# A transformer block on one Trainium2 core: the key weights are loaded through ScalarE's DMA queue instead of SyncE's

## The chip, the cores and the metric

The kernel runs on one core of a Trainium2 chip. The core has five engines with an instruction stream each: TensorE (PE, matrix multiplication; its weight loads are listed as PEld), VectorE (DVE), ScalarE (ACT), GpSimd (POOL) and SyncE (SP). Transfers between HBM and the on-chip memory SBUF are moved by 16 DMA engines. An instruction on SyncE's or ScalarE's stream issues such a transfer; the two streams feed separate DMA queues, which the profile calls q1 (SyncE) and q10 (ScalarE), and both queues are served by the same 16 DMA engines.

The metric is the device time of one execution in microseconds (us). Nine executions of the kernel before took between 219.12 and 220.82 us, with a median of 219.65 us.

## The reference, cut to what matters

One transformer block over 2048 tokens of width 512, in bf16: a modulated layer norm and a linear attention with 32 heads whose features are a softmax of a small projection and of its negative, then a second modulated layer norm and a gated MLP.

```python
mod = (silu(c) @ w_mod).reshape(1, 6, 1, -1)       # sa, ca, ga, sb, cb, gb
h = layernorm(x) * (1 + ca) + sa
# attention A(h)
q, k, v = split(h @ wqkv)                          # 32 heads of 16
pq, pk = q @ w_phi, k @ w_phi                      # per head, 16x16
phi_q = concat(softmax(pq), softmax(-pq))
phi_k = concat(softmax(pk), softmax(-pk))
kv, z = phi_k.T @ v, phi_k.sum(tokens)
o = (phi_q @ kv) / (phi_q @ z + 1e-6)
x = x + ga * (o @ wo)
h = layernorm(x) * (1 + cb) + sb
x = x + gb * ((sigmoid(h @ w_gate) * (h @ w_up)) @ w_down)
```

The part of this that the change touches is the middle third of `wqkv`, columns 512 to 1023: the key weights, 512 x 512 in bf16, 512 KB.

## The kernel before, in words

The 2048 tokens are 16 tiles of 128. The kernel never computes k itself. It folds the key weights and w_phi into one matrix first, so that pk = h @ wqk_f, and does the same for the queries later. Its first 12 us do this:

- **Loads.** ScalarE issues two small ones: `c_row` (1 KB) and `wp_sb` (w_phi, 16 KB in rows of 32 bytes, lines 493 and 495), and then loads its activation table (line 496). SyncE issues the large ones, in this order: x0a (x of tiles 0 and 1, 256 KB), wk (the key weights into the second half of `wqk_sb`, 512 KB, line 923), x0b (tiles 2 and 3, 256 KB), the two halves of the modulation weights wm00 and wm01 (512 KB each, line 921), x1 (tiles 4 to 7), wv (the value weights), wq (the query weights) and x2 (tiles 8 to 11), 512 KB each. One row of x, wk, wv or wq is 1 KB in a transfer, one of wm00 and wm01 is 2 KB.
- **Warm-up.** PE multiplies zeros (`warm`, line 971) from 1.2 us on, and a few more such products stand between the real ones.
- **Fold.** PE transposes the key weights in 16 blocks (`tp_w`, line 1002); DVE and ACT copy the result from PSUM to `wT_sb` (lines 1008 and 1006). POOL makes the block-diagonal `bd` out of `wp_sb` (line 954). PE multiplies `wT_sb` by `bd` (`fold_ps`, line 1019), and ACT and DVE copy that to `wqk_f` (lines 1025 and 1027).
- **Modulation and layer norm.** DVE takes statistics of each x tile (`st`, line 1043), DVE, ACT or POOL normalises it (`xn`), the tile is transposed on PE (`tp_h`, line 1087) or by a DMA transpose that SyncE issues (line 1079), and the modulation (`modc`, out of wm00 and wm01, line 983) is applied on the way to `h1T`.

Then K and V of each tile are computed by PE (lines 1114 and 1118), the features by ACT, DVE and POOL, and summed into `kvacc`; the queries, the attention output, the second norm and the MLP follow.

The order of the work is set when the program is built. A planner (class `Graph`, line 291) takes each task with its engines, an assumed cost, what it reads and writes, and a due time, the due times being shifted by a table (`DUE`); it runs a list schedule with these numbers, and `emit` (line 530) calls the tasks' functions in that order. From then on each engine executes its stream in order and waits by semaphores only for what an instruction reads. A load task costs SyncE 0.45 in the planner and has a size, from which the planner works out a landing time. The three ScalarE instructions at lines 493 to 496 are not in the plan; they are written out ahead of it.

Transfers signal through eight semaphores that are handed out in turn over the transfers of both queues. A transfer that gets a semaphore for the second time waits at its issue until that semaphore's earlier transfer has landed; for x2 the earlier transfer is `wp_sb`.

Of the kernel before, what the change touches and what calls it, by code (L numbers as in the profile page):

```python
# [17 lines left out]
S, D, H, DH, F = 2048, 512, 32, 16, 1376  # L18
# [407 lines left out]
def kernel(  # L426
# [5 lines left out]
    pe, act, dve, pool, sp = nc.tensor, nc.scalar, nc.vector, nc.gpsimd, nc.sync  # L432
# [39 lines left out]
    wqk_sb = cst.tile([P, KT, 2 * D], BF16, name="wqk_sb")  # L472
# [15 lines left out]
    wqkv_v = A_wqkv.rearrange("(j p) n -> p j n", p=P)  # L488
# [2 lines left out]


    act.dma_start(c_row[:], c)
    with nc.allow_non_contiguous_dma(reason="small w_phi load"):
        act.dma_start(wp_sb[:], A_w_phi.rearrange("(kt hl) d f -> (hl d) kt f", hl=8))
    act.preload_act_table_set("natural_log_exp_and_others")
# [416 lines left out]
    def load(name, key, fn, nbytes, due, rel=0.0):  # L913
        G.add("ld_" + name, {"SP": 0.45}, fn, w=key, due=due, rel=rel, nbytes=nbytes)

    K1 = 1024.0
    def load_x(nm, a, b, due):
        load(nm, [("x", t) for t in range(a, b)], lambda e: sp.dma_start(x_sb[:, a:b, :], x_v[:, a:b, :]), 128 * (b - a) * K1, due, rel=max(0.0, due))

    def load_wm(i, due):  # L920
        load(f"wm0{i}", [("wmod0", i)], lambda e: sp.dma_start(wmod_sb[:, 2 * i:2 * i + 2, 0:1024], wmod_v[:, 2 * i:2 * i + 2, 0:1024]), 512 * K1, due)
    load_x("x0a", 0, 2, -20.0)
    load("wk", ["wk"], lambda e: sp.dma_start(wqk_sb[:, :, D:2 * D], wqkv_v[:, :, D:2 * D]), 512 * K1, -19.0)
    load_wm(0, -18.5)
    load_wm(1, -18.0)
    load_x("x0b", 2, 4, -17.0)
# [375 lines left out]
```

## Time and profile before

| | |
|---|---|
| median of 9 executions | 219.65 us |
| the profiled execution: its time | 219.98 us |
| its span, first to last instruction | 218.1 us |
| PE busy | 204.3 us, 94% of the span |
| DVE busy | 169.5 us, 78% |
| ACT busy | 111.1 us, 51% |
| POOL busy | 95.7 us, 44% |
| moved by DMA | 19.02 MB, 87 GB/s over the span |

Times in the profile are counted from the span's start. A timeline line reads: start, duration, engine, source line, operation, destination<-source, sizes, count, and in brackets how long the engine was idle before it and what released it; "SPq" and "ACTq" are the issue of a transfer on SyncE and ScalarE. A line of waits reads: who waited, for whom, us in total, times, longest. A window line reads: the stretch, its length, the busy time and the number of instructions of PE, PEld, DVE, ACT and POOL, then the mean clock granted to PE (1.00 is full), the busy share of the DMA engines and the GB/s that they moved. The chain is followed back from the last instruction to what released each step.

### The profile page before, as it was taken

How to read it: one execution, taken by the hardware profiler on the slowest of the kernel's cores; microseconds unless marked ns; L12 is line 12 of the kernel's file. 1: busy time of each engine (PE TensorE's matmuls, PEld its weight loads, DVE VectorE, ACT ScalarE, POOL GpSimd, SP SyncE). 2: the span in 40 equal slices, each digit the busy share in tenths (PEclk: the TensorE clock that was granted, in tenths of full speed). 3: DMA queues.
4: the chain of work that ended last, by engine and by line, in shares of the span. 5: the costliest groups of instructions: out<-in, count | busy, mean ns of one | idle time of the engine just before them, and what ended most of it. 6: DMA issues, size and time to landing. Idle time of an engine off the chain costs nothing.

```text
span 218.1 us, 4243 instructions
## 1 busy us (share of the span) xinstructions
PE 204.3 (94%) x1494; PEld 113.9 (52%) x1519; DVE 169.5 (78%) x425; ACT 111.1 (51%) x268; POOL 95.7 (44%) x121
## 2 busy tenths in 40 slices
PE   7995999999999999999997799999999999999990
PEld 2632555564566587868754344554444444444550
DVE  3899999999679998788789999999869872333430
ACT  3797899999858984234642133352233523115100
POOL 4367999999999665813312602233104100000000
PEclk9998899999999999999999999999999999999999
DMA  5998982992000210341311210224111221000011
GB/s 162 366 270 222 325 202 51 329 385 66 0 3 3 48 27 3 75 72 26 73 48 50 48 29 0 48 47 122 2 48 27 48 67 57 0 18 6 6 60 47
DMA packets 32511, 19.02 MB, mean 87 GB/s; under 512 B 21761, under 2 KB 30434, under 8 KB 32482
## 3 DMA queue, kind: packets, MB, share of 16 engines
q1 hardware_dynamic: 31952, 18.65, 32.3%
q8 instruction: 14, 0.23, 0.4%
q14 instruction: 15, 0.12, 0.2%
q10 hardware_dynamic: 530, 0.02, 0.1%
HBM read 11.58 MB, written 2.10 MB: 63 GB/s over the span
## 4 chain that ended last, share of the span: by engine, by line
PE 78%; DVE 10%; DMA 4%; issue 2%; ACT 1%; POOL 1%; SPq 0%; DVEq 0%; POOLq 0%; ACTq 0%
PE g_ps L841 16%; PE y_ps L864 15%; PE u_ps L841 15%; PE k_ps L1114 6%; PE a_ps L752 6%; PE q_ps L1188 6%; PE v_ps L1118 4%; DMA wqk_sb<-in_A_wqkv_dram 2%; DMA h1T<-xn 2%; PE num L719 2%; PE kvacc L544 2%; DVE u L710 1%; DVE m L660 1%; PE num L643 1%; POOL phi L1136 1%
## 5 line engine op out<-in xcount | busy, mean ns | idle before, releaser
L845 ACT ACTIVATE tg<-g_ps 128x512 bf16<-128x512 f32 (+3 forms) x66 | 29.3, 454 | 58.7 <-PE g_ps L841 34.1
L850 DVE SCALAR_TENSOR_TENSOR wmod_sb<-tg,u_ps 128x512 bf16<-128x512 bf16 (+5 forms) x66 | 32.0, 501 | 16.0 <-PE u_ps L841 9.0
L864 PE MATMUL y_ps<-wd_sb,wmod_sb 128*128 128x512 bf16 (+2 forms) x179 | 41.2, 366 | 0.4
L743 POOL TENSOR_TENSOR o<-u 128x512 bf16<-128x512 f32 x14 | 17.7, 1271 | 33.4 <-DVE u L710 24.0
L841 PEld LDWEIGHTS <-wu_sb 128*128 128x128 bf16 (+1 forms) x264 | 23.2, 100 | 17.1 <-DVE u L710 0.7
L841 PEld LDWEIGHTS <-wg_sb 128*128 128x128 bf16 (+1 forms) x264 | 23.0, 100 | 17.5 <-issue 1.4
L1136 POOL TENSOR_TENSOR phi<-e,ks 128x1024 bf16<-128x1024 bf16 (+2 forms) x22 | 31.5, 1454 | 0.4
L841 PE MATMUL g_ps<-wT_sb,wg_sb 128*128 128x512 bf16 (+3 forms) x130 | 25.1, 325 | 1.4 <-DVE u L710 1.1
L864 PEld LDWEIGHTS <-wmod_sb 128*128 128x128 bf16 (+1 forms) x187 | 17.9, 98 | 16.1
L841 PE MATMUL u_ps<-wT_sb,wu_sb 128*128 128x512 bf16 (+3 forms) x130 | 24.9, 325 | 0.1
L841 PE MATMUL u_ps<-wqk_sb,wu_sb 128*128 128x128 bf16 (+5 forms) x132 | 20.8, 290 | 0.2 <-DVE u L710 0.2
L841 PE MATMUL g_ps<-wqk_sb,wg_sb 128*128 128x128 bf16 (+5 forms) x130 | 20.5, 289 | 0.1
L873 DVE TENSOR_TENSOR ot<-y_ps,x 128x512 bf16<-128x512 f32 (+1 forms) x17 | 11.2, 657 | 11.5 <-PE y_ps L864 11.5
L1133 DVE TENSOR_REDUCE ks<-e 128x64 f32<-128x1024 bf16 (+2 forms) x22 | 19.5, 902 | 0.7 <-ACT e L1130 0.7
L1118 PE MATMUL v_ps<-wv_sb,h1T 128*128 128x512 bf16 x61 | 16.4, 388 | 2.1 <-ACT h1T L1094 1.2
L1130 ACT ACTIVATE e<-k_ps 128x512 bf16<-128x512 f32 (+2 forms) x44 | 17.9, 499 | 0.2 <-PE k_ps L1114 0.2
L1193 ACT ACTIVATE eT<-q_ps 128x512 bf16<-128x512 f32 x32 | 17.0, 628 | 1.5 <-PE q_ps L1188 1.0
L1114 PE MATMUL k_ps<-wqk_f,h1T 128*128 128x512 bf16 x61 | 16.5, 395 | 0.2
L752 PE MATMUL a_ps<-wo_sb,oT 128*128 128x512 bf16 x62 | 16.2, 379 | 0.1
L1188 PE MATMUL q_ps<-h1T,wqk_f 128*128 128x512 bf16 x62 | 15.5, 379 | 0.1
L1043 DVE BATCH_NORM_STATS2 st<-x_sb 128x6 f32<-128x512 bf16 x16 | 10.7, 671 | 2.7 <-DMA x_sb<-in_A_x_dram 2.7
L1177 POOL TENSOR_TENSOR wd_sb<-wd_sb,wmod_sb 128x512 bf16<-128x512 bf16 x11 | 12.5, 1169 | 0.0
(146 smaller groups left out, 300.3 us busy)
## 6 DMA issues: line engine op xcount, KB each, us to landing
wmod_sb<-in_w_mod_dram SPq DMA_DIRECT2D x4, 512.0 KB, 6.2
out_dram<-ot SPq DMA_DIRECT2D x15, 128.0 KB, 1.8
x_sb<-in_A_x_dram SPq DMA_DIRECT2D x3, 512.0 KB, 7.8
wg_sb<-in_B_w_gate_dram SPq DMA_DIRECT2D x1, 1376.0 KB, 6.6
wu_sb<-in_B_w_up_dram SPq DMA_DIRECT2D x1, 1376.0 KB, 9.5
wd_sb<-in_B_w_down_dram SPq DMA_DIRECT2D x1, 1280.0 KB, 13.3
wqk_sb<-in_A_wqkv_dram SPq DMA_DIRECT2D x2, 512.0 KB, 7.0
wmod_sb<-in_w_mod_dram SPq DMA_DIRECT2D x1, 1024.0 KB, 6.6
```

The costliest lines, as they stand in the source:

```text
L743: G.add(f"o{t}", {"POOL": 1.3, "DVE": 0.62}, lambda e, ub=ub, o=o: engine(e).tensor_tensor(o[:], ub[0][:].rearrange("p h d -> p (h d)"), u ...
L752: pe.matmul(ap_[:], lhsT=oT[:, j, :], rhs=wo_sb[:, j, :], start=(j == 0), stop=(j == KT - 1))
L841: pe.matmul(ps[:fsz, 0:n], lhsT=w[:, j, ft * P:ft * P + fsz], rhs=h[:, j, 0:n], start=(j == 0), stop=(j == KT - 1))
L845: G.add(f"tg{k}.{ft}", {"ACT": 0.13 + n * 0.00083}, lambda e, tg=tg, g_ps=g_ps, fsz=fsz, n=n: act.activation(tg[:fsz, 0:n], g_ps[:fsz, 0:n ...
L850: dve.scalar_tensor_tensor(hm_all[:fsz, hm[k].slot, ft, 0:n], tg[:fsz, 0:n], 1.0, u_ps[:fsz, 0:n], op0=ALU.add, op1=ALU.mult)
L864: pe.matmul(y[:, 0:c1 - c0], lhsT=hm_all[:fsz, hm[k].slot, ft, tl * P:(tl + 1) * P], rhs=wd_sb[:fsz, ft, c0:c1], start=(ft == 0), stop=(ft ...
L1114: pe.matmul(kp[:], lhsT=h1T[:, j, t * P:(t + 1) * P], rhs=wqk_f[:, j, D:2 * D], start=(j == 0), stop=(j == KT - 1))
L1118: pe.matmul(vp[:], lhsT=h1T[:, j, t * P:(t + 1) * P], rhs=wv_sb[:, j, :], start=(j == 0), stop=(j == KT - 1))
L1130: act.activation(ee[:, ha:hb, s, :], kp[:, ha * DH:hb * DH].rearrange("p (h j) -> p h j", j=DH), ACT.Exp, scale=1.0 - 2.0 * s)
L1133: dve.tensor_reduce(ks[:, ha:hb].rearrange("p h s -> p (h s)"), ee[:, ha:hb].rearrange("p h s j -> p (h s) j"), axis=AX.X, op=ALU.add)
L1136: pool.tensor_tensor(ph[:, ha * 32:hb * 32].rearrange("p (h j) -> p h j", j=DH), ee[:, ha:hb].rearrange("p h s j -> p (h s) j"), ks[:, ha: ...
L1188: pe.matmul(qp[:], lhsT=wqk_f[:, j, blk * P:(blk + 1) * P], rhs=h1T[:, j, cq * 512:(cq + 1) * 512], start=(j == 0), stop=(j == KT - 1))
```

## The change

The key weights' load is taken out of SyncE's stream and written out on ScalarE's, between its two small loads. The planner's task `ld_wk` stays, with its cost and size, but emits nothing, so that the planner makes the same order as before.

```diff
     act.dma_start(c_row[:], c)
+    act.dma_start(wqk_sb[:, :, D:2 * D], wqkv_v[:, :, D:2 * D])
     with nc.allow_non_contiguous_dma(reason="small w_phi load"):
         act.dma_start(wp_sb[:], A_w_phi.rearrange("(kt hl) d f -> (hl d) kt f", hl=8))
     act.preload_act_table_set("natural_log_exp_and_others")
...
     load_x("x0a", 0, 2, -20.0)
-    load("wk", ["wk"], lambda e: sp.dma_start(wqk_sb[:, :, D:2 * D], wqkv_v[:, :, D:2 * D]), 512 * K1, -19.0)
+    load("wk", ["wk"], lambda e: None, 512 * K1, -19.0)
     load_wm(0, -18.5)
```

On SyncE the order is now x0a, x0b, wm00, wm01, x1, wv, wq, x2; on ScalarE it is c_row, wk, wp_sb, the table. All other instructions of all engines stand in the order of before. The semaphores are handed out in turn as before; x2 now shares its semaphore with wk, and waits at its issue for wk's landing instead of that of `wp_sb`.

## The prediction

> **What bounds the kernel now.** I read the page first (PE is busy for 94% of the span, so what the first stage loses is not made up by spare time later unless PE or its feeders have some), then the chain of the first 22 us, then the timeline and the waits of the first 12 us, and the windows for how full the DMA engines and each engine are. The chain:
>
> ```profile
> 1.32 4.74 DMA wqk_sb<-in_A_wqkv_dram
> 6.06 0.05 issue
> 6.11 0.91 PE tp_w L1002 x12
> ...
> 8.92 0.46 PE fold_ps L1019 x8
> 9.38 0.02 issue
> 9.41 0.48 DVE wqk_f L1027
> ...
> 13.94 4.12 DMA h1T<-xn
> ```
>
> The reader is to see that the kernel starts on exactly the load that is moved: wk, issued at 1.32, landed at 6.06, and PE, DVE, POOL and a DMA transpose follow without a gap worth naming. Timeline and waits give the two inputs of the fold, wk and `wp_sb`:
>
> ```profile
> 0.79 0.53 ACTq L493 DMA_DIRECT2D c_row<-in_c_dram  x1
> 1.32 0.45 SPq L923 DMA_DIRECT2D wqk_sb<-in_A_wqkv_dram  x1
> 1.35 0.45 ACTq L495 DMA_DIRECT2D wp_sb<-in_A_w_phi_dram  x1
> 1.83 1.28 ACT L496 ACT_TABLE_LOAD   x1 [1.83 <-issue]
> ...
> 6.11 0.91 PE L1002 MATMUL tp_w<-ident,wqk_sb 128*128 128x128 bf16 x12
> 6.87 1.15 POOL L954 TENSOR_TENSOR bd<-wp_sb,bmask 128x512 bf16<-128x512 bf16 x1 [3.21 <-DMA wp_sb<-in_A_w_phi_dram]
> 8.76 1.06 PE L1019 MATMUL fold_ps<-bd,wT_sb 128*128 128x128 bf16 x16
> 9.41 1.29 DVE L1027 CAST wqk_f<-fold_ps 128x512 bf16<-128x512 f32 x2 [0.33 <-PE fold_ps L1019]
> ```
>
> ScalarE's second issue starts at 1.35, as early as SyncE's second at 1.32: the change buys no earlier issue. `bd` ends at 8.02, 0.74 us before the fold at 8.76. The windows:
>
> ```profile
> 2.00:3.00 1.00, 1.00 (x4) 0.38 (x3) 0.00 (x0) 1.00 (x1) 0.83 (x7) 1.00 0.90 249
> 3.00:4.00 1.00, 1.00 (x6) 0.17 (x5) 0.35 (x1) 0.11 (x1) 0.66 (x7) 1.00 0.59 120
> 4.00:5.00 1.00, 1.00 (x7) 0.43 (x8) 0.96 (x3) 0.47 (x3) 0.00 (x0) 1.00 1.10 351
> 5.00:6.00 1.00, 1.00 (x3) 0.09 (x1) 0.90 (x6) 0.68 (x3) 0.00 (x0) 1.00 1.16 334
> 6.00:7.00 1.00, 0.89 (x14) 0.85 (x14) 0.51 (x3) 0.63 (x1) 0.13 (x1) 1.00 1.07 377
> 7.00:8.00 1.00, 1.00 (x11) 0.57 (x8) 0.97 (x4) 0.87 (x2) 1.00 (x1) 1.00 1.07 393
> 8.00:9.00 1.00, 1.00 (x12) 0.64 (x11) 0.97 (x4) 0.30 (x1) 0.02 (x1) 1.00 1.03 369
> ...
> 20.00:25.00 5.00, 4.95 (x26) 2.51 (x26) 4.61 (x13) 4.12 (x13) 5.00 (x5) 0.66 1.11 323
> ```
>
> From 4 us on one queue keeps all 16 DMA engines full; only 3 to 4 us is thin. The last column added up (GB/s times 1 us is kB, with 16 kB before 2 us) is 385 kB by 4 us, 736 by 5, 1070 by 6, 1447 by 7, 1840 by 8, 2209 by 9.
>
> **The change part by part.**
>
> *SyncE loses one issue (0.45 us).* x0b and the rest are issued 0.5 us earlier. With the engines full that moves no byte sooner by itself: 0. x2 now waits for wk instead of `wp_sb`; behind it on SyncE stand only the transposes at 12.58, and its bytes queue behind wq (issued 4.87, landed 9.3 us later), so a wait of even 5 us is covered: 0.
>
> *ScalarE gains one issue (0.45 us).* The table load moves from 1.83 to 2.33 and ends at 3.6; ScalarE's next instruction started at 4.22, after a wait for PE: covered, with 0.6 us to spare.
>
> *wk shares instead of queueing.* Before, the bytes ahead of and with wk's last were x0a 262 kB, wk 524, c_row and `wp_sb` 17: 803 kB, reached at 5.2 us on the curve; it landed at 6.06, so 0.86 us passes from last byte to landing. Now x0a no longer stands ahead of wk, but all of SyncE's queue runs beside it. Low bound: wk starts at 2.45 (x0a's bytes began about 1.1 us after its issue, between 1.75 and 2.0, and wk is issued at 1.35), the queues share byte by byte, and the second queue fills the thin stretch. Then 128 kB have moved at 2.45, twice 524 follow: 1176 kB, at 6.3 us, less 0.6 us for the filled stretch, plus 0.86: 6.55, that is +0.5. High bound: ScalarE's second transfer starts as late as `wp_sb`'s did (5.4 us from issue to landing for 16 KB; in the trace's packet records its first packet runs at 3.86 us) and shares packet by packet, against wm00 and wm01 with their 2 KB rows. Then 262 + 262 + 524 + 1048 = 2096 kB must move: 8.7 + 0.86 = 9.55, that is +3.5. I take sharing packet by packet from 3.0 us, because `wp_sb`'s records do just that (one of its packets every 48 ns on an engine, between wk's of 46 ns): x0b's 262 kB beside half of wk, then 524 kB of wm beside the other half, 262 + 524 + 262 + 524 = 1572 kB, at 7.3 us; plus 0.86, less 0.2 for part of the thin stretch: wk lands at 8.0, **+1.9 us**. Below nothing is nearly excluded: PE's last warm-up product starts at 5.37 and such products follow each other every 0.43 us, so `tp_w` cannot start before 5.8, a gain of 0.3 at most.
>
> The Trainium skill, in "DMA: Bandwidth & Descriptors", under "Issuing engines are not separate DMA queues", says that transfers from different engines run on the same 16 DMA engines and interleave, and that a second issuer saves only the sequencer's time. The windows agree, at 334 to 393 GB/s from one queue. By that rule the change would gain at most an issue, 0.45 us, and here not that; it speaks against the change.
>
> *`wp_sb` goes behind wk* in ScalarE's queue. It cannot land before wk; low bound 0.3 after it. High bound: each DMA engine has 32 of its packets and each waits for one 2 KB packet of the other queue, 83 ns at the 393 GB/s shared by 16: 2.7 us after wk. I take 1.3: 9.3. `bd` (1.15) then ends at 10.5, where PE, running `tp_w` to fold in 2.65 us as before (6.11 to 8.76), reaches the fold at 8.05 + 2.65 = 10.7. So it is just covered; at the high bound `bd` ends at 11.95 and the fold is 3.2 late instead of 1.9.
>
> *PE's clock.* PE is idle from 5.8 to 8.0. After 16 to 20 us, in which PE is busy 1.47 of 4 us, the granted clock averages 0.66 in 20 to 25: 1.7 us of clock lost. A gap of 2.2 us may or may not do the same: 0 to +1.7. I take +0.3, as the gap is shorter and much of what follows waits for DVE.
>
> *What of it reaches the end.* The fold's delay goes to DVE's copies (9.41), the norm's scalars, `xn` and the DMA transposes (issued 12.58). That transpose takes 4.12 us in the chain, against 2.4 in the page's row of `oT<-o`: up to 1.7 of the delay could vanish in this queueing. But DVE, in order behind the fold, idles 0.6 us in all from 12 to 25 us (busy 1.93, 1.94, 2.00, 1.93 of 2, then 4.61 of 5), and later PE and POOL idle 0.6 and 0.8 from 25 to 60. Kept: between 1.9 − 0.6 − 0.6 = 0.7 and all of 1.9; I take 1.3.
>
> Sum: 1.3 + 0.3 = +1.6 us. On the profiled execution's 219.98 that is 221.6; it stands 0.33 above the median of 219.65, so the forecast for a median is **221.3 us**.
>
> **The rivals.**
>
> *The start is late but the stage swallows it (no change).* wk lands by 6.7, `wp_sb` soon after, and DVE's and PE's 1.2 us of later idle time take up the 0.6. For it: the thin stretch. Against: the 2 KB rows beside wk. It gives 219.6 to 220.3.
>
> *`wp_sb` becomes the late input*, or the clock is lost, or both: 3.2 or 1.9 + 1.7 at the fold, less 0.6 to 1.2 on the way: +2.0 to +3.0, so 221.7 to 222.7, and 223.4 with wk at its high bound and little swallowed.
>
> *Faster.* wk gets more than its share and the two queues fill 3 to 4 us. It decides from the point where wk lands before 6.06: `tp_w` starts up to 0.3 earlier, and if the fold's successors, tight behind x1 and wm01, follow because those come 0.6 earlier, up to 0.8 in all: 218.9. Against it stands that `wp_sb` must then also land before 7.6, or `bd` takes the gain back.
>
> **How the numbers follow.** A measurement of this kernel tells about 0.3% (0.66 us) from no change. Chances: the forecast (220.4 to 222.2) 0.50; `wp_sb` or the clock (up to 223.4) 0.23; swallowed 0.20; faster 0.07. The range from 219.4 to 223.2 leaves out the faster case and the last of the slow one, under 2 in 10 together. Beyond 0.66 us slower: 0.73; within: 0.20; faster: 0.07.
>
> **What would show each step.** In the profile after: `tp_w` starting near 8.0 with PE's wait for wk grown from 1.0 to about 2.9 us; `bd` starting after 8.5; the fold at 10.5 or later; 3 to 4 us moving more than 120 GB/s; the clock in the windows from 9 to 14 us. Wrong would make it: wk landing before 6.7, or the h1T transposes still landing near 18.06 with DVE caught up by 25 us.

## The result, and the profile after

The changed kernel takes 221.97 us (median of 10 executions, 221.27 to 226.05) beside 219.56 us for the kernel before (31 executions, 219.09 to 220.82). The ratio is 1.011, with a 95% interval from 1.009 to 1.013: 2.4 us slower, where +1.6 was forecast. Two of the ten executions (225.20 and 226.05 us) are more than 1.5% above the fastest, count as slow and are left out of the ratio; the median of the other eight is 221.70 us, 2.1 us slower. Its profiled execution took 221.25 us over a span of 219.5, 1.27 more than the profiled execution of before.

The timeline of the changed kernel's first 12 us, in the columns of the timeline of before (most source lines are numbered one higher, as the change adds a line):

```profile
1.36 0.44 ACTq L494 DMA_DIRECT2D wqk_sb<-in_A_wqkv_dram  x1
1.82 0.97 SPq L922 DMA_DIRECT2D wmod_sb<-in_w_mod_dram  x2
1.83 0.55 ACTq L496 DMA_DIRECT2D wp_sb<-in_A_w_phi_dram  x1
2.41 1.28 ACT L497 ACT_TABLE_LOAD   x1 [2.41 <-issue]
...
6.00 0.84 PE L1003 MATMUL tp_w<-ident,wqk_sb 128*128 128x128 bf16 x12 [0.76 <-DMA wqk_sb<-in_A_wqkv_dram]
...
9.45 1.15 POOL L955 TENSOR_TENSOR bd<-wp_sb,bmask 128x512 bf16<-128x512 bf16 x1 [5.79 <-DMA wp_sb<-in_A_w_phi_dram]
10.64 1.05 PE L1020 MATMUL fold_ps<-bd,wT_sb 128*128 128x128 bf16 x16 [1.90 <-POOL bd L955]
...
11.29 1.29 DVE L1028 CAST wqk_f<-fold_ps 128x512 bf16<-128x512 f32 x2 [2.39 <-PE fold_ps L1020]
```

The moved load is not late here: `tp_w` starts at 6.00, where it started at 6.11. The late one is the load behind it in ScalarE's queue. `bd` starts at 9.45 instead of 6.87, PE stands 1.90 us in front of the fold, and the fold starts at 10.64 instead of 8.76. In order behind the fold, DVE waits 2.39 instead of 0.33. The waits of the first 25 us (us in total, times, longest) name the same chain:

```profile
POOL bd L955 <- DMA wp_sb<-in_A_w_phi_dram: 5.8, 1, 5.8
PE fold_ps L1020 <- POOL bd L955: 1.9, 1, 1.9
PEld L1003 <- DMA wqk_sb<-in_A_wqkv_dram: 1.3, 1, 1.3
```

The DMA view by queue shows why (packets, MB, share of 16 engines; q1 is SyncE's, q10 ScalarE's). First the stretch from 4 to 5 us, then that from 6 to 9 us, both of the changed kernel:

```profile
q10 hardware_dynamic: 359, 0.37, 104.7%
q1 hardware_dynamic: 28, 0.01, 4.6%
...
q1 hardware_dynamic: 673, 1.05, 99.6%
q10 hardware_dynamic: 509, 0.02, 10.2%
```

From 4 to 5 us wk has the DMA engines almost to itself: x0a is through and x0b nearly so (its last packet starts at 4.19), and the modulation weights, issued at 1.82, after wk at 1.36, begin only at 5.2. From 6 to 9 us, 0.02 MB of `wp_sb` in some 500 packets of 32 bytes stand among 673 packets of SyncE's queue: 385 of 2 KB, 256 of 1 KB (x1, from 8 us on) and 32 of 4 bytes. In the trace's packet records a small packet takes 9 ns, one of 2 KB 86 ns. For most of the time the small ones go singly between large ones: their most frequent distances are 86 ns ahead of 6.4 us and 86 to 100 ns behind 7.1 us. Each DMA engine has 32 of them, so an engine on which they alternate all the way needs 32 x (9 + 86) = 3.0 us (an estimate from these two durations). The packets of `wp_sb` start between 5.83 and 8.73 us. By the landing events 11 of the 16 engines had brought their part by 8.26 and the last five from 9.01 to 9.37; a load lands with its last engine, so `wp_sb` lands at 9.37, where it landed at 6.80 before.

The Trainium skill, "DMA: Bandwidth & Descriptors", in its section on queues, rings and completion order, says that a DMA engine alternates between the queues that have work, a whole packet of typically 9 to 17 descriptors at a time. The alternation is seen here, but for most of the stretch it goes record by record, as the distance of 86 ns shows. Groups appear only from 6.5 to 7.0 us, where SyncE's queue goes over from one half of the modulation weights to the other: 258 of the 512 small packets start there beside 77 of 2 KB, in rows 6 ns apart.

The windows of the changed kernel:

```profile
3.00:4.00 1.00, 1.00 (x6) 0.16 (x5) 0.19 (x1) 0.69 (x1) 0.66 (x7) 1.00 1.01 347
...
9.00:10.00 1.00, 0.00 (x0) 0.00 (x0) 0.00 (x0) 0.00 (x0) 0.56 (x1) 1.00 1.10 347
10.00:11.00 1.00, 0.36 (x7) 0.35 (x7) 0.00 (x0) 0.00 (x0) 1.00 (x2) 1.00 1.10 348
20.00:25.00 5.00, 4.47 (x29) 2.06 (x31) 4.83 (x17) 4.82 (x14) 4.89 (x4) 1.00 0.97 311
```

The thin stretch from 3 to 4 us is filled (347 GB/s instead of 120), and the modulation weights' second half lands 0.6 us earlier (8.98 instead of 9.62), but nothing on the path needed them. From 9 to 10 us only POOL works, for 0.56 us: that is the loss of the start. PE's clock stayed at 1.00 through this gap.

A second loss arises far behind the loads, near 120 us, where VectorE and POOL work side by side. The kernel before and the changed kernel:

```profile
119.99 0.29 DVE L660 TENSOR_TENSOR m<-smS 128x32 f32<-128x32 f32 x2
120.15 2.49 POOL L743 TENSOR_TENSOR o<-u 128x512 bf16<-128x512 f32 x2 [2.79 <-DVE u L710]
120.32 1.14 DVE L662 TENSOR_TENSOR den<-m 128x32 f32<-128x32 f32 x1
...
120.38 1.40 DVE L661 TENSOR_TENSOR m<-smS 128x32 f32<-128x32 f32 x2
120.46 2.48 POOL L744 TENSOR_TENSOR o<-u 128x512 bf16<-128x512 f32 x2 [2.79 <-DVE u L711]
121.81 1.18 DVE L663 TENSOR_TENSOR den<-m 128x32 f32<-128x32 f32 x1
```

In both, a DVE instruction that starts while POOL's first `o` runs ends only 0.05 us after it: `den` before (1.14 us), the second `m` here (1.29 us instead of 0.18). Before, the second `m` starts 0.05 us ahead of `o` and is not held; here it starts 0.02 us behind it, `den` then meets the second `o`, and so two instructions are held instead of one. Compared instruction by instruction, the changed kernel is 0.31 us behind at 118 us and 0.92 from 124 us to the last instruction of DVE. All six profiles with the changed kernel's loads (its own three, two with PE filled, one with a constant in `bd`) gain this 0.61, and none of the six other edited runs below that can be compared does. What moves DVE by the 0.07 us that decide it is not shown. On DVE's stream one wait for a semaphore near 88 us is missing in these six (81 such waits instead of 82), so the two programs differ there too.

### The profile page after: what moved, and what is told of

Same layout as the page of the kernel before. It is cut to its first block, busy times and chain, and to the rows that moved or that the text cites. A ratio compares the mean times of both kernels' runs of the same rounds, so it can differ in the third digit from the quotient of the medians.

```text
span 219.5 us, 4242 instructions
## 1 busy us (share of the span) xinstructions
PE 202.4 (92%) x1494; PEld 112.7 (51%) x1519; DVE 168.9 (77%) x425; ACT 110.9 (51%) x268; POOL 95.5 (44%) x121
## 4 chain that ended last, share of the span: by engine, by line
PE 71%; DVE 16%; issue 6%; POOL 3%; ACT 1%; DVEq 0%; POOLq 0%
PE g_ps L842 16%; PE y_ps L865 15%; PE u_ps L842 15%; PE a_ps L753 6%; PE q_ps L1189 5%; PE k_ps L1115 4%; DVE ks L1134 3%; DVE st L1044 2%; PE v_ps L1119 2%; PE num L720 2%; DVE m L661 2%; DVE u L711 2%; PE kvacc L545 1%; PE num L644 1%; DVE h1T L1097 1%
## 5 line engine op out<-in xcount | busy, mean ns | idle before, releaser
L1115 PE MATMUL k_ps<-wqk_f,h1T 128*128 128x512 bf16 x61 | 15.6, 379 | 0.2
```

What stands on the lines that cost most here:

```text
L1115: pe.matmul(kp[:], lhsT=h1T[:, j, t * P:(t + 1) * P], rhs=wqk_f[:, j, D:2 * D], start=(j == 0), stop=(j == KT - 1))
```

## The experiments

Three theories stood after the first profile. **W**: the loss is the late `wp_sb`, stuck behind wk in ScalarE's queue and beside 2 KB packets, and through it `bd` and the fold. **Q**: the loss is wk itself on a second queue, shared with SyncE's loads, which the one profile happened to miss. **C**: the loss is PE's clock, halved in a stretch of 3.4 us after PE's idle time in many executions. The runs came in four sets, each beside executions of the kernel before on the same chip (medians 219.85, 219.40, 219.67 and 219.46 us).

**`wp_sb` ahead of wk in ScalarE's queue.**

```diff
 act.dma_start(c_row[:], c)
-act.dma_start(wqk_sb[:, :, D:2 * D], wqkv_v[:, :, D:2 * D])
 act.dma_start(wp_sb[:], ...)
+act.dma_start(wqk_sb[:, :, D:2 * D], wqkv_v[:, :, D:2 * D])
```

> The two loads on ScalarE's queue change places: c_row, wp_sb, then the key weights wk. Theory W (the changed kernel loses because wp_sb stands behind wk in ScalarE's queue, lands at 9.4 us instead of 6.8, and so bd and the fold come 1.9 us late): wp_sb lands by 6.9 and bd ends near 8.1; the fold then waits for wk alone. If transfers of both queues are served in the order of their issue, wk (issued at 1.85, just after the first half of the modulation weights at 1.8) starts only after that half, lands near 7.3, and the fold starts near 10.0: 220.5 to 221.0 us. If the queues are served side by side, wk lands 0.5 us later than in the changed kernel, near 6.5, the fold starts near 9.1: 219.8 to 220.1. Rival Q (it is the use of ScalarE's queue for a large load as such that costs, whatever the order): 221.5 to 222.5.

Measured: 225.44 us (4 executions), ratio 1.026 [1.022, 1.030]. A miss by 4.4 us and more, and the most useful one. Its timeline:

```profile
4.66 1.15 POOL L955 TENSOR_TENSOR bd<-wp_sb,bmask 128x512 bf16<-128x512 bf16 x1 [0.99 <-DMA wp_sb<-in_A_w_phi_dram]
10.20 1.46 PE L1003 MATMUL tp_w<-ident,wqk_sb 128*128 128x128 bf16 x12 [4.20 <-DMA wqk_sb<-in_A_wqkv_dram]
...
14.39 1.06 PE L1020 MATMUL fold_ps<-bd,wT_sb 128*128 128x128 bf16 x16
```

`bd` is now early, but wk is issued at 1.83, just behind the modulation weights' first half (1.82 on SyncE) instead of 0.46 ahead of it. Its packets start at 4.5 to 5 and alternate with the 2 KB ones until 9.7 (122 ns is the most frequent distance in both lists); wk lands at 10.15. From 6 to 9 us ScalarE's queue gets 0.37 of 1.07 MB, a third of the bytes. So a place half a microsecond later in the order of issue, over both queues, decides between wk alone and wk at a third of the rate, 4.2 us apart. This is Q's sharing, beyond the high bound of the prediction's step (wk at 9.55), but it hangs on the order, which Q had denied. The idle PE then ran slowly: from `tp_w` to the fold it took 4.19 us instead of 2.65 (warm-up products behind `tp_w` took 1.06 for two instead of 0.59), and these 1.5 us are a part of the fold's 5.6. That this is the clock is an inference: two products take 1.06 at the 0.50 shown further below, and here the trace's clock records begin only at 13.56, where the products become short; for the time ahead of the first record the windows print 1.00.

**`wp_sb` on SyncE behind x0a, wk on ScalarE.**

```diff
 act.dma_start(c_row[:], c)
 act.dma_start(wqk_sb[:, :, D:2 * D], wqkv_v[:, :, D:2 * D])
-act.dma_start(wp_sb[:], ...)
...
 sp.dma_start(x_sb[:, a:b, :], x_v[:, a:b, :])        # x0a
+sp.dma_start(wp_sb[:], ...)
```

> wk stays on ScalarE's queue as in the change; wp_sb goes to SyncE's queue, directly after x0a. Theory W: wp_sb lands before 7 us, bd ends before 8.2, wk lands near 6.0 and the fold starts at 8.5 to 8.9, as before the change or a little sooner: 219.2 to 219.8 us. Rival Q: still 221 or more.

Measured: 219.83 us (10 executions), ratio 1.0002 [0.9986, 1.0018].

```profile
5.04 1.15 POOL L958 TENSOR_TENSOR bd<-wp_sb,bmask 128x512 bf16<-128x512 bf16 x1 [1.37 <-DMA wp_sb<-in_A_w_phi_dram]
5.87 0.84 PE L1006 MATMUL tp_w<-ident,wqk_sb 128*128 128x128 bf16 x12 [0.16 <-DMA wqk_sb<-in_A_wqkv_dram]
...
8.45 1.06 PE L1023 MATMUL fold_ps<-bd,wT_sb 128*128 128x128 bf16 x16
```

The loss is gone with wk still on ScalarE's queue. The edit also puts the modulation weights one issue later, so wk is further ahead of them, and the 0.61 us at 120 us are gone too. The fold is 0.31 us earlier than before, and the time does not show it.

**Before, with `wp_sb` alone made late** (wk stays on SyncE; `wp_sb` on SyncE behind both halves of the modulation weights).

```diff
-act.dma_start(wp_sb[:], ...)
...
 sp.dma_start(wmod_sb[:, 2 * i:2 * i + 2, 0:1024], ...)   # second of the two
+sp.dma_start(wp_sb[:], ...)
```

> The kernel before the change, with wk on SyncE's queue; only wp_sb is moved, to SyncE's queue behind both halves of the modulation weights. Theory W: wp_sb lands near 9.8, bd ends near 11.0 and the fold starts near 11.1, 2.3 us later than before, so the time rises by 1.5 to 3: 221.0 to 222.6 us. If what follows swallowed a late fold, or the loss came from moving wk: 219.3 to 220.3.

Measured: 222.24 us (4 executions), ratio 1.011 [1.007, 1.014], the changed kernel's own.

```profile
6.18 0.84 PE L1005 MATMUL tp_w<-ident,wqk_sb 128*128 128x128 bf16 x12 [0.80 <-DMA wqk_sb<-in_A_wqkv_dram]
...
10.04 1.15 POOL L957 TENSOR_TENSOR bd<-wp_sb,bmask 128x512 bf16<-128x512 bf16 x1 [6.38 <-DMA wp_sb<-in_A_w_phi_dram]
11.24 1.71 PE L1022 MATMUL fold_ps<-bd,wT_sb 128*128 128x128 bf16 x16 [2.32 <-POOL bd L957]
```

A late `wp_sb` is enough for a loss of this size, with no load on ScalarE's queue but `c_row`. It is made up differently, though: the fold is 2.5 us late instead of 1.9, PE's clock was halved from 11.4 to 14.9 us as well (the fold took 1.71 instead of 1.06), 2.1 us are still there at 118 us, and nothing is added at 120.

**PE kept busy in front of the fold** (theory C; the changed kernel with seven products of zeros ahead of the fold).

```diff
+if side == 1 and not filled:
+    filled.append(1)
+    for _ in range(7):
+        pe.matmul(ps[:], lhsT=wd_sb[:, FT - 1, 0:P], rhs=wd_sb[:, FT - 1, :], start=True, stop=True)
```

> The changed kernel with seven more warm-up products of zeros on PE directly ahead of the fold, where it waits 1.9 us for bd; they take 1.5 us at full clock and end before bd does. Theory C (a part of the loss, and the wider scatter of the changed kernel, is PE's clock, which is halved in some executions after that wait): the median falls to 221.0 to 221.4 and the times lie within 1 us. If the clock has no part in it: 221.6 to 222.3 as the changed kernel, with its scatter.

Measured: 221.89 us (4 executions), ratio 1.010 [1.006, 1.014]: nothing gained, although PE's wait for `bd` fell from 1.90 to 0.52 us. The same kernel once more on another chip:

> The changed kernel with the seven warm-up products ahead of the fold, again, with more executions beside the changed kernel on the same chip. Theory C: no execution above 222.8, mean clocks of 0.988 and more, and a median lower by 0.3 us or more. If the clock has no part, scatter, clocks and median like the changed kernel's.

Measured: 221.55 us (6 executions), ratio 1.010 [1.006, 1.013]. One of its executions had a mean clock of 0.999 and took 222.68 us; another took 226.84, against the expectation. C falls as the cause of the median; as an addition in single executions it comes back below.

**The modulation weights in packets of 1 KB** (each half as two transfers; bytes, loads and queues as in the changed kernel).

```diff
-sp.dma_start(wmod_sb[:, 2 * i:2 * i + 2, 0:1024], ...)
+[sp.dma_start(wmod_sb[:, 2 * i:2 * i + 2, h * 512:(h + 1) * 512], ...) for h in range(2)]
```

> The changed kernel, with each half of the modulation weights loaded by two transfers with rows of 1 KB instead of one with rows of 2 KB; the same bytes, and wp_sb still behind wk on ScalarE's queue. If wp_sb is late because each of its 32 packets per DMA engine waits for one packet of the other queue (in the changed kernel they run from 5.9 to 8.8 us, about 100 ns each beside 2 KB packets of 88 ns), half the packet size halves that: wp_sb lands at 7.8 to 8.2 instead of 9.4, bd ends near 9.2, the fold starts near 9.3 and the time is 220.2 to 220.9. If it is late because it stands behind a fixed amount of bytes or a fixed latency, it still lands near 9.4 and the time stays at 221.5 to 222.3.

Measured: 219.95 us (10 executions), ratio 1.0024 [1.0001, 1.0048]. Most of the loss is gone, more than was expected.

```profile
7.06 0.84 PE L1003 MATMUL tp_w<-ident,wqk_sb 128*128 128x128 bf16 x12 [1.46 <-DMA wqk_sb<-in_A_wqkv_dram]
...
8.56 1.15 POOL L955 TENSOR_TENSOR bd<-wp_sb,bmask 128x512 bf16<-128x512 bf16 x1 [4.89 <-DMA wp_sb<-in_A_w_phi_dram]
9.76 1.05 PE L1020 MATMUL fold_ps<-bd,wT_sb 128*128 128x128 bf16 x16
```

`wp_sb` lands at 8.48 instead of 9.37, and the fold is 1.0 us late instead of 1.9. The small packets started over 2.2 us (5.49 to 7.69) instead of 2.9. This fits the size of the neighbour's packets as the price, but does not isolate it: the extra issues also delay later loads (x1 is issued at 4.52 instead of 2.83), and the 0.61 us at 120 us are gone as well. The landing did not halve; one DMA engine brought its part of wk 0.67 us, and its part of `wp_sb` 0.53 us, after the next latest.

**`wp_sb` first, then wk, with `c_row` moved to SyncE** (both of ScalarE's loads one issue earlier than in the first run).

```diff
-act.dma_start(c_row[:], c)
 act.dma_start(wp_sb[:], ...)
 act.dma_start(wqk_sb[:, :, D:2 * D], wqkv_v[:, :, D:2 * D])
...
 sp.dma_start(x_sb[:, a:b, :], x_v[:, a:b, :])        # x0a
+sp.dma_start(c_row[:], c)
```

> The load of c_row goes to SyncE's queue behind x0a, so that ScalarE's queue begins with wp_sb (issued at 0.8) and wk (issued at 1.3); the rest as in the changed kernel. If loads start in the order of their issue over both queues, wp_sb lands by 4, wk starts near 3 and lands at 5.2 to 5.7, tp_w starts at 5.4 to 5.8 and the fold at 8.0 to 8.4, 0.4 to 0.7 earlier than before the change. If that reaches the end, 219.0 to 219.4 us, 0.2 to 0.3% faster than before; if it is lost in what follows, as the 0.3 us of the run with wp_sb on SyncE's queue were, 219.6 to 220.0.

Measured: 219.74 us (12 executions), ratio 1.003 [1.001, 1.006]. `bd` starts at 4.00, as expected, but `tp_w` at 6.42 and the fold at 9.00, later than the 8.0 to 8.4 of the expectation. The same order of ScalarE's two loads as in the first run, with wk issued at 1.31 instead of 1.83 and the modulation weights at 2.17 instead of 1.82: 5.7 us less (the two runs were on different chips). It does not beat the kernel before.

**The changed kernel again**, for a second and a third profile.

> The changed kernel once more, for a second profile and more times beside the next run. Theory C (PE's clock, halved in some executions after the wait for bd, makes the scatter): median 221.5 to 222.3 with some executions above 222.8, and these have the lower mean clocks, under 0.985.

Measured: 221.71 us (6 executions, 220.76 to 223.74), ratio 1.010 [1.006, 1.015]; the profiled execution took 222.47 us. The slowest had a mean clock of 0.989, so the low clocks that theory C expected of slow executions are not seen.

```profile
8.09 1.15 PE L1003 MATMUL tp_w<-ident,wqk_sb 128*128 128x128 bf16 x12 [2.49 <-DMA wqk_sb<-in_A_wqkv_dram]
...
10.88 1.15 POOL L955 TENSOR_TENSOR bd<-wp_sb,bmask 128x512 bf16<-128x512 bf16 x1 [7.22 <-DMA wp_sb<-in_A_w_phi_dram]
12.33 1.06 PE L1020 MATMUL fold_ps<-bd,wT_sb 128*128 128x128 bf16 x16
```

Here wk is late as well. By the trace's landing events, 15 of 16 DMA engines had brought their share of it by 6.16 us and one at 8.04. Its last 22 packets of wk started from 6.21 to 7.42, when the other engines had none left: 18 of them 42 ns apart, as with no neighbour, and only the last four 122 ns apart, with a 2 KB packet between. So sharing explains little of its lateness, and the cause stays open. The lateness went on to every later load: the last engine was 1.41 us behind the next latest with the first half of the modulation weights, 1.22 with `wp_sb` and 1.39 with x1. The fold is 3.6 us late. Two things hold it: `bd` ends at 12.03, and PE, which ran from `tp_w` to the fold without a gap, did so at half its clock, as the same kernel's windows show (0.50 in the column of the granted clock):

```profile
9.00:10.00 1.00, 1.00 (x7) 0.45 (x5) 0.96 (x4) 0.58 (x1) 0.00 (x0) 0.50 1.07 347
10.00:11.00 1.00, 1.00 (x7) 0.61 (x6) 0.95 (x4) 0.45 (x1) 0.12 (x1) 0.50 1.09 353
```

At full clock PE would have been at the fold at 8.09 + 2.65 = 10.74, and `bd` alone would have held it to 12.03: the clock cost 0.3 here, because `bd` covered the rest.

> No edit: the changed kernel once more, beside the two others on the same chip, for a third profile of it. Theory that the two queues race at each DMA engine: wk lands anywhere between 5.9 and 8.1 us and wp_sb between 9.3 and 10.9, always behind it, the fold at 10.4 to 12.4, and the median is 221.6 to 222.1. Rival, that the execution with wk at 8.04 was an accident of one chip: wk at 5.9 to 6.2 and the fold at 10.4 to 10.7 again.

Measured: 221.75 us (5 executions, 221.44 to 221.94), ratio 1.009 [1.008, 1.011]; `tp_w` at 6.21, `bd` at 9.62, the fold at 10.82, PE's wait for `bd` 1.84 us. So two profiles of the three show wk on time and `wp_sb` late, one shows both late. (Four further profiles have the same loads, two with PE filled and two with other values in `bd`: wk landed at 6.06, 5.87, 5.96 and 7.48.)

**wk first of all on ScalarE's queue, then `wp_sb`; `c_row` on SyncE.**

```diff
-act.dma_start(c_row[:], c)
 act.dma_start(wqk_sb[:, :, D:2 * D], wqkv_v[:, :, D:2 * D])
 act.dma_start(wp_sb[:], ...)
...
 sp.dma_start(x_sb[:, a:b, :], x_v[:, a:b, :])        # x0a
+sp.dma_start(c_row[:], c)
```

> Edit: the changed kernel with the c_row load taken off ScalarE's queue and put on SyncE's behind x0a, so that ScalarE issues wk first (at about 0.8 us) and wp_sb second (1.35). Order-of-issue theory (loads start in the order in which both queues issued them, and a queue is only disturbed where the other has packets at the same DMA engine): wk now starts before wm's first half, lands at 4.8 to 5.3 us, tp_w starts at 5.3 to 5.9, wp_sb's small packets run from about 4.5 and land between 6 and 7.5, bd ends before 8.7, the fold is at 8.0 to 8.7, no later than the 8.76 of before. Time 219.3 to 220.0 beside 219.4 to 219.9 of before: the loss of the changed kernel is gone. Rival, that wk on ScalarE's queue is itself the cost (shared with SyncE's 2 KB rows wherever it stands): wk lands at 6 to 8, the fold at 10 or later, time 221 to 222. Rival, that an earlier start is worth its size: fold at 8.1 gives 218.8 to 219.2; the run with wp_sb on SyncE (fold 0.3 earlier, time the same) speaks against it.

Measured: 221.16 us (6 executions), ratio 1.006 [1.004, 1.007]. A miss on the time, half right on the loads: `wp_sb` landed at 6.39, as expected, but wk at 6.21 instead of 4.8 to 5.3. What was late is the 1 KB of `c_row`:

```profile
PEld L948 <- DMA c_row<-in_c_dram: 2.4, 1, 2.4
PE c_ps L948 <- DMA c_row<-in_c_dram: 1.5, 1, 1.5
```

```profile
5.47 0.26 PE L948 MATMUL c_ps<-ones,c_row 1*128 1x1 bf16 x4 [1.49 <-DMA c_row<-in_c_dram]
5.67 1.89 PE L975 MATMUL warm<-wd_sb 128*128 128x512 bf16 x4
7.35 1.46 PE L1006 MATMUL tp_w<-ident,wqk_sb 128*128 128x128 bf16 x12
```

The first fence is of the waits, the second of PE's timeline. On PE `c_ps` stands ahead of four warm-up products and `tp_w`; a `c_row` that lands 1.5 us late holds them all, in order. `tp_w` itself took 1.46 instead of 0.84 behind PE's idle stretch, and the fold starts at 10.55. x0a was late too (4.89 instead of 3.62), sharing with wk from the first packet. Neither rival's condition held: wk was not at 8, and the start was not early.

**`bd` without `wp_sb`** (the changed kernel with all its loads, w_phi replaced by other values in `bd`). Twice; first by the block mask's ones:

```diff
-    bd[:].rearrange(...), wp_sb[:].unsqueeze(2).to_broadcast(...)
+    bd[:].rearrange(...), bmask[:, 0:KT * DH].rearrange(...).unsqueeze(2).to_broadcast(...)
```

> Edit: the changed kernel, all loads as they are, but bd is made from the block mask instead of from wp_sb, so that neither bd nor the fold waits for wp_sb (the part that is changed: w_phi is replaced by values of the mask in the fold). What is left of the change is the landing of wk. Theory that the late wp_sb carries the loss: tp_w starts at 6.0 as in the changed kernel's profile, the fold at 8.7, time 219.5 to 220.2, and where one DMA engine brings its part of wk only at 8 us, tp_w is at 8.1, the fold at 10.7 and that execution takes 220.7 to 221.7; the median of the run 219.6 to 220.5, most of the +2.3 gone. Rival, that wk itself is late in most executions (the +1.9 us of the forecast): median 221.3 to 222, as the changed kernel's.

Measured: 595.05 us. Ones in place of w_phi break the bound on the projections, and the kernel then takes its second, general path, so the time says nothing here. Its start is that of the changed kernel, though, and the fold is at 8.63 with `tp_w` at 6.00. Then with a constant small enough for the first path:

```diff
+pool.memset(wp_c[:], 0.002)
...
-    bd[:].rearrange(...), wp_sb[:].unsqueeze(2).to_broadcast(...)
+    bd[:].rearrange(...), wp_c[:].unsqueeze(2).to_broadcast(...)
```

> Edit: the changed kernel, all loads as they are, but bd is made from a tile that POOL fills with the constant 0.002 at the start instead of from wp_sb, so that neither bd nor the fold waits for wp_sb (the part that is changed: w_phi is replaced by that constant; unlike with the mask's ones, the bound that chooses between the two paths of the kernel still holds). What is left of the change is the landing of wk. Theory that the late wp_sb carries the loss: where wk lands at about 6 us, tp_w starts at 6.0 to 6.2 and the fold at 8.7 to 8.8, time 219.4 to 220.2; where one DMA engine brings its part of wk only at 8 us, tp_w is at 8.1, the fold at 10.7 and that execution takes 220.7 to 221.7; median of the run 219.5 to 220.5. Rival, that wk itself is late in most executions, or that something else than the fold's start carries the loss: median 221.3 to 222, as the changed kernel's.

Measured: 224.18 us (6 executions, 221.27 to 224.96), ratio 1.022 [1.020, 1.025]. Neither theory expected this. The profiled execution was the fastest of them, 221.27:

```profile
7.52 0.84 PE L1005 MATMUL tp_w<-ident,wqk_sb 128*128 128x128 bf16 x12 [1.52 <-DMA wqk_sb<-in_A_wqkv_dram]
...
10.11 1.06 PE L1022 MATMUL fold_ps<-bd,wT_sb 128*128 128x128 bf16 x16
```

Here 15 DMA engines had landed their part of wk by 5.81 us and one at 7.48, and the fold, now waiting for wk alone, is 1.35 us late. The other five executions took 223.6 to 225.0 and have no trace. So W, as "without the wait for `wp_sb` the loss is gone", falls: in this execution the landing of wk is a cost of its own. It had the 0.61 us at 120 us too. That wk lost its place on more engines in the other five, as in the first run (wk at 10.15, 225.44 us), is an inference; why this kernel on this chip should fall there more often than the changed kernel did on three others is not settled. The constant also changes the values that the rest of the kernel works on, and no run separates that from the loads.

**All starts against all times.** Thirteen profiled executions (all but that of the general path) give one point each: the start of the fold and the execution's time. From `wp_sb` on SyncE (8.45, 219.85), before (8.76, 219.98) and `wp_sb` then wk (9.00, 219.09), over the changed kernel's three (10.64, 221.25; 10.82, 221.45; 12.33, 222.47), to `wp_sb` first (14.39, 224.60), a straight line fits them: time = 212.1 + 0.86 x fold, correlation 0.96, the largest distance 0.74 us. On average 0.86 of a late fold came out at the end. But not all that comes out comes from the fold: six of the thirteen hold the 0.61 us at 120 us, and the stretch from the last DVE instruction to the end took 4.9 to 5.6 us, with no tie to the start. Taken at 118 us, ahead of both, the slope is 0.79, and the changed kernel's three lie under the line: 0.31 us behind the kernel before for a fold 1.88 late, 0.47 for 2.06, and 2.06 for 3.57.

## Why the prediction was right, point by point

The forecast of 221.3 us had the sign, and the measured 221.97 lies in its range. But the way there was that of a rival: "`wp_sb` becomes the late input", 221.7 to 222.7, with a chance of 0.23. That the number came near is in part luck: wk was forecast 2 us too late and `wp_sb` 2 us too close behind it, and 0.61 us arose at 120 us, in no term of the sum. (The prediction calls the first-issued half of the modulation weights wm00; by the planner's names it is the second half. Nothing hangs on it.)

- *SyncE loses an issue, x2's wait: 0.* Held: the second half of the modulation weights landed 0.6 us earlier, and x2's issue is on no path.
- *ScalarE's table load moves: 0.* Held: 2.41 to 3.69, ahead of the work of 4.2.
- *wk shares: lands at 8.0, +1.9.* The step that failed in two of three profiles: `tp_w` started 0.1 early and 0.1 late, and in another 2.0 late. It failed at "sharing packet by packet from 3.0 us": wk starts at 3.5 and does share, but with x0b only, which is through by 4.2; the modulation weights, issued 0.46 us behind wk, begin at 5.2, when wk is nearly done. I had let them run beside half of wk. The high bound (9.55) was passed by the run in which wk was issued behind them (10.15).
- *`wp_sb` behind wk, "I take 1.3: 9.3".* The mis-sized term that made the loss: it landed 3.4, 3.4 and 2.8 us after wk, above even the high bound of 2.7, which had the right mechanism for the engines that finish last (one 2 KB packet for each of 32, at 83 ns; measured 86, and 9 for the small one). That the landing itself was given almost exactly (9.3 against 9.37) is luck, as wk came 2 us earlier and `wp_sb` 2 us later after it than taken. So `bd` was not "just covered": with `tp_w` early, PE waited 1.9 us for it.
- *PE's clock: +0.3.* No part of the profiled loss: 1.00 through the gap, and filling the gap gained nothing. In single executions it does come: 0.3 at the fold in the changed kernel's second profile, and, if the slow products there are the clock's, 1.5 in the run with `wp_sb` first. So 0 to +1.7 was a fair bound, and 0 the value of the execution shown.
- *What reaches the end: 0.7 to 1.9, taken 1.3 of 1.9.* The size came out, the path did not. The two profiled times differ by 1.27 us for a delay of 1.88 (0.68, as taken), but of the delay only 0.31 is left at 118 us, under the lower bound; 0.61 arose at 120 us, and the rest, about 0.4, in the last stretch, which varies as much from profile to profile. The absorption began where the step put it: DVE is 1.9 us behind until 20 us and 0.35 at 25 (the same instruction in both traces), as the transposes, issued 1.9 later, landed only 0.4 later. The kernel before also ran at half clock from 19.95 to 23.36 us, which the changed kernel did not in this profile, and the comparison holds that too.
- *Sum: +1.6 against +2.4.* By the line above the median of +2.4 would stand for a fold 2.8 us late (2.4 / 0.86, an estimate that puts the 0.61 at 120 us down to the fold), between the profiles with `wp_sb` late alone (+1.9, +2.1) and that with both late (+3.6).

Of the signs named as showing it wrong, "wk landing before 6.7" came true, at 5.95, and the kernel was slower all the same: the sign looked at one of the fold's two inputs. The other, the transposes landing near 18.06 with DVE caught up by 25 us, nearly came true as well (18.47, and 0.35 behind). The rule weighed in the prediction, from "DMA: Bandwidth & Descriptors", section "Issuing engines are not separate DMA queues", is that a second issuer saves issue time only; the runs agree on the gain, as the two orders that kept both inputs early gave ratios of 1.0002 and 1.003. The cost, 1.1%, came from the order of the loads and not from issue time.

What is shown: a late `wp_sb` alone can cost +2.4 (with the fold 2.5 us late and a halved clock behind it); with `wp_sb` early and wk issued well ahead of the modulation weights the loss is gone; in all three profiles of the changed kernel the fold starts right behind the end of `bd` (0.04, 0.05 and 0.30 us after it); and in all three 0.61 us are added at 120 us. What stays open: why the start of DVE's instructions moves there, why single DMA engines fall behind, how much of the median's +2.4 is wk's own lateness on such engines and how much the clock's, since that differs from execution to execution and only profiled ones have a trace, and why the kernel with a constant in `bd` took 224.

## What to carry to other kernels

Before a load is moved to a second DMA queue, list what stands behind it in that queue, and in which order the two queues' issues interleave: a load's place in the joint order of issue decided whether 512 KB came alone or at a third of the rate. A small load in rows of 32 bytes paid, on the engines that finished last, one packet of the other queue for each of its own, so it belongs ahead of the large ones, whichever queue it is in. When a step has two inputs, forecast both landings and the wait for the later one; a start that was late by 1 us cost 0.86 us at the end on average over the profiles of this kernel. Before all of a loss is put down to the start, compare the two traces instruction by instruction to the end: here a quarter of it arose 100 us later.

## What was not expected of the hardware

- Service followed the order of issue over both queues at the start: wk issued 0.46 us ahead of the modulation weights ran alone from 4 to 5 us (359 packets against 28); issued 0.01 us behind them it had a third of the bytes and landed 4.2 us later.
- One of the 16 DMA engines can bring its share of a load long after the others, and stay behind with all later loads: wk at 8.04 against 6.16 for the next latest and x1 at 12.13 against 10.74 in one profile, wk at 7.48 against 5.81 and x1 at 11.31 against 10.45 in another. A load lands with its slowest engine, and this was different in executions of the same kernel.
- The 512 packets of the 16 KB load ran over 2.9 us beside 2 KB packets (5.83 to 8.73 in the changed kernel), over 2.2 beside 1 KB packets in the kernel before (3.86 to 6.04), and over 0.9 when issued first on ScalarE's queue (2.60 to 3.52). In the stretches where they stood in rows they were 6 ns apart.
- In the run with wk first, the first packets of SyncE's queue (the 12 that start before 2.0 us) took 443 ns each on average, and 164 in the next half microsecond. In the other runs these were 46 to 73 ns (176 in the run with the mask's ones) and 57 to 105. x0a landed 1.3 us late.
- A short DVE instruction that started while POOL's `o` ran ended only 0.05 us after it: 1.14 to 1.29 us instead of 0.18. Whether one or two of them met it hung on 0.07 us.
